# Expert steps 36 to 39 of a routed expert kernel put under run-time conditions on the number of steps in use

## The chip, the core and the metric

One core of one Trainium2 chip runs the whole program. The metric is the device time of one execution in microseconds; the kernel before has a median of 1045.79 us over three runs.

## What is computed

The input is q, k and v for 8 batches, 8 heads, 576 positions and 64 features per head. Attention acts within chunks of 64 positions. Its output, 4608 tokens of 512 features, goes through a router that sends each token to one of 8 experts, and through that expert's two layers. All data are fp32.

```python
# attention, per chunk of 64
scores = scale * q_c @ k_c.T;  attn = softmax(scores);  out = attn @ v_c
# bridge: (B, H, S, D) -> x of (4608, 512)
logits = normalised(x) @ normalised(expert_emb).T / tau
expert_idx = argmax(logits);  gate_w = probs[expert_idx]
for e in range(8):
    mask = expert_idx == e
    out[mask] = gate_w[mask] * (relu(x[mask] @ w1[e]) @ w2[e])   # 512 -> 1024 -> 512
```

## The kernel before

The program has three stages on the core. The **attention stage** works through 36 tiles of 128 tokens; it also forms the router's logits, and writes the attention output to the DRAM tensor `x_rows`. The **seam** sorts the tokens: it gives each token a block of 64 tokens of one expert, and each block a place in a step. The **expert stage** runs steps.

A step holds two blocks, one in each half of 128 rows. The blocks are numbered by expert; half 0 takes them from the front and half 1 from the back, so that `mid`, half the number of blocks rounded up, is the number of steps that have a block (lines 367 and 368). How many blocks there are depends on the data: 4608 tokens are 72 full blocks, and each expert's last block may be partly filled. The fixed number of steps is `NST = NT + E // 2` = 36 + 4 = 40. Steps from `mid` on hold padding: their gather reads row 0, and their scatter rows are out of range, so that nothing is written.

The seam also makes two small tables on one partition: `eblk`, the expert of each half in each step, and `fresh`, which is 1 where a step's expert differs from that of the step two before. SP reads both (`number`, line 483) and issues a weight load of a step and half only where `fresh` is set (`load_w`, line 494). Each weight buffer is double, by the step's parity.

A step consists of these parts:

- `gather` (line 513): POOL fetches 128 rows of `x_rows` by an indirect DMA, four steps ahead.
- `turn_xb` (line 525): PE transposes the rows, DVE copies them to `xbT` (line 531).
- `hidden` (line 534): 16 matmul calls of 512 columns, 32 instructions in the profile, on the first layer (line 541); DVE applies the relu to the first half of h (line 552) and ACT to the second (line 550).
- `turn_h` (line 555): eight transposes of h on PE (line 562), copied to `hT` by DVE (line 566) and ACT (line 564).
- `result` (line 569): 16 matmul calls on the second layer (line 574); ACT scales by the gate (line 582) and POOL scatters the rows to the output (line 583).

The order of the work is written out by hand (`manual_schedule`), and each engine runs its instructions in that order. The loop at line 604 is a software pipeline: in its turn j, PE does `hidden` of step j + 1, `turn_h` of j, `turn_xb` of j + 2 and `result` of j - 1. Nearly every wait of PE for DVE or ACT is thus filled with another step's matmuls. SP's queue holds the weight loads in the same order; a load waits until the matmuls that read its buffer are done.

Of the kernel before, what the change touches and what calls it, by code (L numbers as in the profile page):

```python
# [11 lines left out]
I32 = mybir.dt.int32  # L12
AF = mybir.ActivationFunctionType
ALU = mybir.AluOpType
AX = mybir.AxisListType
PSUM = bass.MemoryType.PSUM
ENG = mybir.EngineType
# [8 lines left out]
def kernel(  # L26
# [11 lines left out]
    nc = tc.nc  # L38
# [7 lines left out]
    NT = N // P  # L46
    NCB = S // CH
    G = P // 2
    NST = NT + E // 2
# [4 lines left out]
    keep = ctx.enter_context(tc.tile_pool(name="keep", bufs=1))  # L54
# [12 lines left out]
    gate_at = keep.tile([P, NST], FP32, name="gate_at")  # L67
    eblk = keep.tile([1, 2, NST], I32, name="eblk")
    fresh = keep.tile([1, 2, NST], I32, name="fresh")

    make_identity(nc, ident)

# [213 lines left out]
    with (  # L286
# [7 lines left out]
        io = sp.tile([P, P], FP32, name="io")  # L294
# [66 lines left out]
        mid = sp.tile([P, 1], FP32, name="mid")  # L361
# [28 lines left out]
        for i in range(2):  # L390
            nc.vector.tensor_scalar(
                fresh[:, i, 0:2], e_of[:, i, 0:2], float((0, E - 1)[i]), None, ALU.not_equal
            )
        nc.vector.tensor_tensor(
            fresh[:, :, 2:NST], e_of[:, :, 2:NST], e_of[:, :, 0 : NST - 2], ALU.not_equal
        )


# [75 lines left out]
    with (  # L474
# [5 lines left out]
    ):  # L480
        xin, mo = {}, {}

        def number(ap, top, engine):
            return nc.values_load(
                ap,
                engines=(engine,),
                min_val=0,
                max_val=top,
                skip_runtime_bounds_check_because="a count of comparisons, less than this",
            )  # L490
# [3 lines left out]
        def load_w(buf, rows, n, s, j):  # L494

            if (s, j) not in new:
                new[s, j] = (
                    number(eblk[0:1, s, j : j + 1], E - 1, ENG.SP),
                    number(fresh[0:1, s, j : j + 1], 1, ENG.SP),
                )  # L500
            e, f = new[s, j]
            nc.sync.dma_start(out=buf[s][j % 2], in_=rows[:, ds(e * n, n), :], cond=f > 0)

        def load_w1(j):
            for s in range(2):
                load_w(w1_sb, w1_rows, KD, s, j)

        def load_w2(j):
            for s in range(2):
                load_w(w2_sb, w2_rows, KF, s, j)  # L510
                del new[s, j]

        def gather(j):
            t = bp.tile([P, D], FP32, tag="xin", name="xin", bufs=XBUF)
            nc.gpsimd.indirect_dma_start(  # L515
                out=t,
                out_offset=None,
                in_=x_rows,
                in_offset=bass.IndirectOffsetOnAxis(ap=src_row[:, j : j + 1], axis=0),
                bounds_check=N - 1,  # L520
                oob_is_err=False,
            )
            xin[j] = t

        def turn_xb(j):
            t = xin.pop(j)
            ps = ps_x.tile([P, KD, P], FP32, tag="x", name="x_ps")
            for c in range(KD):
                nc.tensor.transpose(ps[:, c], t[:, c * P : c * P + P], ident)
            xT = bp.tile([P, KD, P], FP32, tag="xbT", name="xbT")  # L530
            nc.vector.tensor_copy(xT, ps)  # L531
            mo[j] = {"xT": xT}

        def hidden(j):
            d = mo[j]
            h = bp.tile([P, F], FP32, tag="h", name="h")
            for fh in range(F // 512):
                ps = ps_h.tile([P, 512], FP32, tag="h", name="h_ps")
                for c in range(KD):
                    for s in range(2):  # L540
                        nc.tensor.matmul(  # L541
                            ps[G * s : G * s + G],
                            lhsT=d["xT"][:, c, G * s : G * s + G],
                            rhs=w1_sb[s][j % 2][:, c, fh * 512 : fh * 512 + 512],
                            start=(c == 0),
                            stop=(c == KD - 1),
                        )
                dst = h[:, fh * 512 : fh * 512 + 512]
                if fh % 2:
                    nc.scalar.activation(dst, ps, AF.Relu)  # L550
                else:
                    nc.vector.tensor_scalar(dst, ps, 0.0, None, ALU.max)  # L552
            d["h"] = h

        def turn_h(j):
            d = mo[j]
            hT = bp.tile([P, KF, P], FP32, tag="hT", name="hT")
            for g in range(KF // 4):
                ps = ps_ht.tile([P, 4, P], FP32, tag="ht", name="ht_ps")
                for c in range(4):  # L560
                    f0 = (4 * g + c) * P
                    nc.tensor.transpose(ps[:, c], d["h"][:, f0 : f0 + P], ident)  # L562
                if g % 2:
                    nc.scalar.copy(hT[:, 4 * g : 4 * g + 4], ps)
                else:
                    nc.vector.tensor_copy(hT[:, 4 * g : 4 * g + 4], ps)  # L566
            d["hT"] = hT

        def result(j):
            d = mo.pop(j)  # L570
            ps = ps_y.tile([P, D], FP32, tag="y", name="y_ps")
            for c in range(KF):
                for s in range(2):
                    nc.tensor.matmul(  # L574
                        ps[G * s : G * s + G],
                        lhsT=d["hT"][:, c, G * s : G * s + G],
                        rhs=w2_sb[s][j % 2][:, c],
                        start=(c == 0),
                        stop=(c == KF - 1),
                    )  # L580
            y = bp.tile([P, D], FP32, tag="y", name="y", bufs=3)
            nc.scalar.activation(y, ps, AF.Copy, scale=gate_at[:, j : j + 1])  # L582
            ins = nc.gpsimd.indirect_dma_start(  # L583
                out=out,
                out_offset=bass.IndirectOffsetOnAxis(ap=dst_row[:, j : j + 1], axis=0),
                in_=y,
                in_offset=None,
                bounds_check=N - 1,
                oob_is_err=False,
            )  # L590
            tc.declare_no_dep(ins.ins, group="rows", reason="blocks hold different tokens")
            tc.add_to_no_dep_group("rows", ins.ins)
# [8 lines left out]
        hidden(0)  # L601
        load_w1(2)
        turn_xb(1)
        for j in range(NST + 1):
            if j + 1 < NST:
                hidden(j + 1)
                if j + 3 < NST:
                    load_w1(j + 3)
            if j < NST:
                turn_h(j)  # L610
            if j + 2 < NST:
                turn_xb(j + 2)
            if j > 0:
                result(j - 1)
                if j + 1 < NST:
                    load_w2(j + 1)
            if j + XBUF < NST:
                gather(j + XBUF)


# [26 lines left out]
```

## Time and profile before

| | |
|---|---|
| three runs | 1044.2, 1045.79, 1046.27 us; median 1045.79 |
| the profiled execution, in all | 1047.4 us |
| its span, first to last instruction | 1045.6 us |
| mean granted TensorE clock | 0.82 |
| PE busy | 907.6 us (87% of the span) |
| DVE, ACT, POOL busy | 268.5, 173.1, 103.9 us |
| DMA | 142.58 MB |

The profile is of one execution. PE is TensorE's matmuls and PEld its weight loads, DVE VectorE, ACT ScalarE, POOL GpSimd and SP the queue that issues weight loads. Times count from the start of the span. The granted clock is a share of full speed: 1.00 is 2.4 GHz and 0.50 is 1.2 GHz. L574 is line 574 of the kernel before. The busy share of the whole span says little here, since the attention stage, the seam and the expert stage have different limits; the rows below are therefore read by stretch.

### The profile page before, as it was taken

Reading aid. Unit: us, or ns where it says so; the run is one execution under the profiler, and the core shown is the slowest. Engines: PE = TensorE matmul, PEld = TensorE weight load, DVE = VectorE, ACT = ScalarE, POOL = GpSimd, SP = SyncE. Lnnn points to the kernel's source line nnn. Section 1 sums busy time; section 2 is a strip of 40 time slices with the busy share of each in tenths; the row PEclk is TensorE's granted clock in tenths of the full one; section 3 lists DMA queues with packets and bytes.
Section 4 is the critical chain, followed back from the end, with each engine's and each line's share of the span. In section 5 each row is a group of like instructions: output and inputs, shape, how many; then the busy total and the mean of one; then the engine's idle time right before and its main releaser. Section 6 shows DMA issues by size and latency. Waiting matters only on the chain.

```text
span 1045.6 us, 15287 instructions
## 1 busy us (share of the span) xinstructions
PE 907.6 (87%) x6287; PEld 485.3 (46%) x6287; DVE 268.5 (26%) x508; ACT 173.1 (17%) x310; POOL 103.9 (10%) x128
## 2 busy tenths in 40 slices
PE   4777777767777745899999999999999999999998
PEld 4666666656666635333333333333333333333332
DVE  3444444343444466111111111111111111111110
ACT  3222222222222220011111011011111101101111
POOL 0000000000000000101111101101110110111101
PEclk9855555555555555899999999999999999999999
DMA  8555465457374100101013575167942142316670
GB/s 204 147 150 168 113 185 171 116 162 200 88 207 133 40 21 1 51 19 41 21 41 121 202 261 202 41 226 285 345 162 106 51 186 106 121 41 233 229 256 2
DMA packets 153670, 142.58 MB, mean 136 GB/s; under 512 B 115702, under 2 KB 115702, under 8 KB 153600
## 3 DMA queue, kind: packets, MB, share of 16 engines
q1 hardware_dynamic: 144256, 112.21, 34.6%
q0 software_dynamic: 9344, 29.39, 7.9%
q8 instruction: 50, 0.82, 0.3%
q14 instruction: 20, 0.16, 0.0%
HBM read 391.14 MB, written 19.92 MB: 393 GB/s over the span
## 4 chain that ended last, share of the span: by engine, by line
issue 56%; PE 21%; DVE 14%; POOL 5%; ACT 2%; POOLq 0%; DMA 0%; SPq 0%
PE lg_ps L226 6%; PE tr L136 6%; PE sc L154 4%; POOL xin L515 4%; PE tr L181 3%; DVE mx L162 2%; DVE a L164 2%; DVE qT L141 2%; DVE rs L172 2%; ACT a L170 2%; DVE xT L220 2%; POOL out_dram L583 2%; PE inv L451 1%; DVE rs L173 1%; DMA kx<-in_k_dram 0%
## 5 line engine op out<-in xcount | busy, mean ns | idle before, releaser
L541 PE MATMUL h_ps<-w,xbT 128*64 128x512 f32 x1280 | 284.5, 597 | 2.4 <-DVE xbT L531 2.4
L574 PE MATMUL y_ps<-w,hT 128*64 128x512 f32 x1280 | 283.3, 595 | 0.0
L541 PEld LDWEIGHTS h_ps<-w,xbT 128*64 128x64 f32 x1280 | 92.3, 138 | 186.5 <-issue 183.3
L574 PEld LDWEIGHTS y_ps<-w,hT 128*64 128x64 f32 x1280 | 88.5, 137 | 167.0 <-issue 167.0
L552 DVE TENSOR_SCALAR h<-h_ps 128x512 f32<-128x512 f32 x40 | 27.7, 692 | 377.9 <-PE h_ps L541 377.9
L226 PE MATMUL lg_ps<-enT,xT 128*128 128x8 f32 x288 | 64.2, 352 | 62.3 <-DVE xT L220 62.3
L583 POOL DMA_INDIRECT out_dram<-y,dst_row x40 | 40.6, 1014 | 532.6 <-ACT y L582 517.2
L226 PEld LDWEIGHTS lg_ps<-enT,xT 128*128 128x128 f32 x288 | 60.8, 312 | 69.2 <-DVE xT L220 69.1
L582 ACT ACTIVATE y<-y_ps,gate_at 128x512 f32<-128x512 f32 x40 | 27.5, 688 | 272.9 <-PE y_ps L574 272.9
L550 ACT ACTIVATE h<-h_ps 128x512 f32<-128x512 f32 x40 | 23.9, 598 | 285.1 <-PE h_ps L541 285.1
L154 PE MATMUL sc<-kT,qT 64*64 64x64 f32 x1152 | 40.7, 317 | 31.5 <-DVE qT L141 31.5
L566 DVE COPY hT<-ht_ps 128x512 f32<-128x512 f32 x40 | 27.7, 692 | 136.6 <-PE ht_ps L562 136.6
L141 DVE COPY qT<-tr 128x512 f32<-128x512 f32 x36 | 24.9, 691 | 136.5 <-PE tr L136 136.5
L154 PEld LDWEIGHTS sc<-kT,qT 64*64 64x64 f32 x1152 | 35.0, 218 | 44.9 <-issue 42.4
L209 POOL DMA_DIRECT2D x_rows<-x x36 | 19.6, 544 | 352.3 <-DVE x L202 352.3
L562 PEld LDWEIGHTS ht_ps<-ident,h 128*128 128x128 f32 x320 | 34.3, 140 | 32.5 <-issue 32.5
L515 POOL DMA_INDIRECT xin<-x_rows,src_row x40 | 41.0, 1024 | 49.5 <-DVE dst_row L465 37.6
L170 ACT ACTIVATE a<-a 128x512 f32<-128x512 f32 x36 | 22.7, 630 | 132.5 <-DVE a L164 132.5
L562 PE MATMUL ht_ps<-ident,h 128*128 128x128 f32 x320 | 43.7, 280 | 0.0
L194 PE MATMUL sc<-v,aT 64*64 64x64 f32 x1152 | 40.8, 318 | 0.0
L136 PE MATMUL tr<-ident,kx 128*128 128x128 f32 x144 | 36.4, 405 | 4.9 <-DMA kx<-in_k_dram 4.9
L218 PE MATMUL tr<-ident,x 128*128 128x128 f32 x144 | 40.0, 433 | 0.0
(118 smaller groups left out, 605.4 us busy)
## 6 DMA issues: line engine op xcount, KB each, us to landing
w<-in_moe_w_dram SPq DMA_DIRECT2D x168, 2048.0 KB
v<-in_v_dram SPq DMA_DIRECT2D x64, 144.0 KB
x_rows<-x POOLq DMA_DIRECT2D x36, 256.0 KB, 2.3
qx<-in_q_dram SPq DMA_DIRECT2D x32, 256.0 KB
kx<-in_k_dram SPq DMA_DIRECT2D x32, 256.0 KB
qx<-in_q_dram SPq DMA_DIRECT2D x8, 128.0 KB
kx<-in_k_dram SPq DMA_DIRECT2D x8, 128.0 KB
xin<-x_rows,src_row POOLq DMA_INDIRECT x40, 3.5
```

The source lines that it names most:

```text
L136: nc.tensor.transpose(ps[:, i], a[:, i * P : i * P + P], ident)
L141: nc.vector.tensor_copy(x, ps)
L154: nc.tensor.matmul(sc[CH * c : CH * c + CH, par, i], lhsT=qx[r0 : r0 + CH, i, c0 : c0 + CH], rhs=kx[r0 : r0 + CH, i, c0 : c0 + CH], start= ...
L170: nc.scalar.activation(a, a, AF.Exp, scale=scale)
L194: nc.tensor.matmul(pv[CH * c : CH * c + CH, par, i], lhsT=d["aT"][r0 : r0 + CH, i, CH * c : CH * c + CH], rhs=v_t[b][r0 : r0 + CH, i, cb], ...
L218: nc.tensor.transpose(ps[:, c], d["x"][:, c * P : c * P + P], ident)
L226: nc.tensor.matmul(lg_ps[:, t], lhsT=d["xT"][:, c], rhs=enT[:, c], start=(c == 0), stop=(c == KD - 1),)
L515: nc.gpsimd.indirect_dma_start(out=t, out_offset=None, in_=x_rows, in_offset=bass.IndirectOffsetOnAxis(ap=src_row[:, j : j + 1], axis=0), ...
L541: nc.tensor.matmul(ps[G * s : G * s + G], lhsT=d["xT"][:, c, G * s : G * s + G], rhs=w1_sb[s][j % 2][:, c, fh * 512 : fh * 512 + 512], sta ...
L562: nc.tensor.transpose(ps[:, c], d["h"][:, f0 : f0 + P], ident)
L574: nc.tensor.matmul(ps[G * s : G * s + G], lhsT=d["hT"][:, c, G * s : G * s + G], rhs=w2_sb[s][j % 2][:, c], start=(c == 0), stop=(c == KF ...
L583: ins = nc.gpsimd.indirect_dma_start(out=out, out_offset=bass.IndirectOffsetOnAxis(ap=dst_row[:, j : j + 1], axis=0), in_=y, in_offset=Non ...
```

## The change

The seam now also keeps `mid` as an integer, `n_steps`, and multiplies `fresh` by `used`, which is 1 for steps below `mid`. The pipelined loop covers steps 0 to 35 (`LEAST = NT` = 36); its prefetches of weights and its gathers still reach into the steps behind it. After the loop, all five engines load `n_steps` into a register. Then step 36 stands in a condition on `n_steps > 36`, and inside it, behind step 36, step 37 in a condition on `n_steps > 37`, and so on to 39. In a condition the parts of a step follow each other without another step's work between them.

```diff
+    n_steps = keep.tile([1, 1], I32, name="n_steps")
...
+        used = sp.tile([1, NST], I32, name="used")
+        nc.vector.tensor_scalar(used, io[0:1, 0:NST], mid[0:1], None, ALU.is_lt)
+        nc.vector.tensor_copy(n_steps, mid[0:1])
         nc.vector.tensor_tensor(
             fresh[:, :, 2:NST], e_of[:, :, 2:NST], e_of[:, :, 0 : NST - 2], ALU.not_equal
+        )
+        nc.vector.tensor_tensor(
+            fresh, fresh, used.unsqueeze(1).to_broadcast([1, 2, NST]), ALU.mult
         )
...
-        def number(ap, top, engine):
+        def number(ap, top, *engines):
             return nc.values_load(
                 ap,
-                engines=(engine,),
+                engines=engines,
...
-        for j in range(NST + 1):
-            if j + 1 < NST:
+
+        LEAST = NT
+        for j in range(LEAST + 1):
+            if j + 1 < LEAST:
                 hidden(j + 1)
                 if j + 3 < NST:
                     load_w1(j + 3)
-            if j < NST:
+            if j < LEAST:
                 turn_h(j)
-            if j + 2 < NST:
+            if j + 2 < LEAST:
                 turn_xb(j + 2)
             if j > 0:
                 result(j - 1)
...
+        steps = number(n_steps, NST, ENG.PE, ENG.DVE, ENG.Activation, ENG.Pool, ENG.SP)
+
+        def more(j):
+            with tc.If(steps > j):
+                turn_xb(j)
+                hidden(j)
+                if j + 2 < NST:
+                    load_w1(j + 2)
+                turn_h(j)
+                result(j)
+                if j + 2 < NST:
+                    load_w2(j + 2)
+                if j + 1 < NST:
+                    more(j + 1)
+
+        more(LEAST)
```

The added lines shift the numbers behind them: what was L531, L541, L550, L552, L562, L564, L566, L574, L582 and L583 is L538, L548, L557, L559, L569, L571, L573, L581, L589 and L590 in the changed kernel.

On PE, where x of step 36 is turned, the order before is this; `h_ps` is written by the matmuls of `hidden` (here of step 35), `ht_ps` by the transposes of h (step 34), and `y_ps` by `result` (step 33):

```order
L541 MATMUL h_ps<-w_01_61,xbT 64x512
L541 MATMUL h_ps<-w_11_63,xbT 64x512
L562 MATMUL ht_ps<-ident,h 128x128 x8
L529 MATMUL x_ps<-ident,xin 128x128 x4
L574 MATMUL y_ps<-w_01_65,hT 64x512
L574 MATMUL y_ps<-w_11_67,hT 64x512
```

In the changed kernel it is this, the first two rows being the last ones of result 35:

```order
L581 MATMUL y_ps<-w_01_65,hT 64x512
L581 MATMUL y_ps<-w_11_67,hT 64x512
L491 TENSOR_LOAD n_steps
L632 COMPARE_AND_BRANCH
L536 MATMUL x_ps<-ident,xin 128x128 x4
L548 MATMUL h_ps<-w_00_60,xbT 64x512
L548 MATMUL h_ps<-w_10_62,xbT 64x512
```

The transposes of step 36's x moved from between two other steps' matmuls to behind the last result of the loop, a register load and a branch, and its `hidden` follows them directly.

In the seam on DVE, the order before and then that of the change (`io` counts 0, 1, 2, ... along a row, `e_of` holds the experts of the steps):

```order
L391 TENSOR_SCALAR fresh<-e_of 1x2 x2
L394 TENSOR_TENSOR fresh<-e_of 1x2x38
L403 TENSOR_TENSOR w<-rank,off 128x288
L404 TENSOR_TENSOR w<-w,eq 128x288
L405 TENSOR_REDUCE dest<-w 128x36
```

```order
L392 TENSOR_SCALAR fresh<-e_of 1x2 x2
L396 TENSOR_SCALAR used<-io,mid 1x40
L397 CAST n_steps<-mid 1x1
L398 TENSOR_TENSOR fresh<-e_of 1x2x38
L401 TENSOR_TENSOR fresh<-fresh,used 1x80
L410 TENSOR_TENSOR w<-rank,off 128x288
L411 TENSOR_TENSOR w<-w,eq 128x288
L412 TENSOR_REDUCE dest<-w 128x36
```

Three operations on one partition now stand ahead of the chain from `w` on.

At the program's end on POOL, before and then in the changed kernel:

```order
L515 DMA xin<-x_rows,src_row 128x512
L583 DMA out_dram<-y,dst_row 4608x512 x5
L642 UNCONDITIONAL_BRANCH
L642 ISA
```

```order
L522 DMA xin<-x_rows,src_row 128x512
L590 DMA out_dram<-y,dst_row 4608x512
L491 TENSOR_LOAD n_steps
L632 COMPARE_AND_BRANCH
L590 DMA out_dram<-y,dst_row 4608x512
L632 COMPARE_AND_BRANCH
L590 DMA out_dram<-y,dst_row 4608x512
```

Of the five scatters behind the last gather, one is left ahead of the register load, and each of the four others stands behind a branch of its own. The part for a condition that does not hold stands further down: it sets the semaphores to what the skipped steps would have left, and branches to the end of the program.

## Rows read from the trace of the kernel before

**Rows 1.** Busy time by stretch: us, PE, PEld, DVE, ACT, POOL, PEclk, DMA share, GB/s

```profile
433.00:450.00 17.00, 15.43 (x78) 5.71 (x76) 3.46 (x5) 1.62 (x3) 0.00 (x0) 1.00 0.00 1
450.00:1000.00 550.00, 550.00 (x2726) 208.07 (x2726) 74.54 (x108) 67.41 (x108) 72.43 (x71) 1.00 0.41 146
```

**Rows 2.** Timeline of the last steps: start us, duration us, engine, line, operation

```profile
987.39 1.09 PE L562 MATMUL ht_ps<-ident,h 128*128 128x128 f32 x8
...
987.58 0.60 ACT L550 ACTIVATE h<-h_ps 128x512 f32<-128x512 f32 x1 [6.22 <-PE h_ps L541]
988.14 0.69 DVE L566 COPY hT<-ht_ps 128x512 f32<-128x512 f32 x1 [3.32 <-PE ht_ps L562]
...
995.77 7.04 PE L541 MATMUL h_ps<-w,xbT 128*64 128x512 f32 x32
...
1018.08 1.09 PE L562 MATMUL ht_ps<-ident,h 128*128 128x128 f32 x8
...
1027.14 13.95 PE L574 MATMUL y_ps<-w,hT 128*64 128x512 f32 x64
```

**Rows 3.** The same view, POOL alone, 1000 us to the end

```profile
1012.32 1.00 POOL L583 DMA_INDIRECT out_dram<-y,dst_row  x1 [14.33 <-ACT y L582]
...
1042.16 0.98 POOL L583 DMA_INDIRECT out_dram<-y,dst_row  x1 [5.93 <-ACT y L582]
```

**Rows 4.** DMA, 1011 to 1020 us: packets, MB, share; issues, us to landing

```profile
q1 hardware_dynamic: 1047, 2.11, 69.4%
q0 software_dynamic: 80, 0.13, 3.8%
...
out_dram<-y,dst_row POOLq DMA_INDIRECT x1, 6.8
```

**Rows 5.** The same view, 1035 to 1040 us

```profile
q0 software_dynamic: 80, 0.00, 0.8%
...
out_dram<-y,dst_row POOLq DMA_INDIRECT x1, 2.1
```

**Rows 6.** Timeline at the head of the expert stage, PE and DVE

```profile
441.94 0.60 PE L529 MATMUL x_ps<-ident,xin 128*128 128x128 f32 x4
...
442.57 0.69 DVE L531 COPY xbT<-x_ps 128x512 f32<-128x512 f32 x1 [0.18 <-PE x_ps L529]
443.32 7.09 PE L541 MATMUL h_ps<-w,xbT 128*64 128x512 f32 x32 [0.78 <-DVE xbT L531]
...
450.34 1.09 PE L562 MATMUL ht_ps<-ident,h 128*128 128x128 f32 x8
```

**Rows 7.** Busy time by stretch, columns as in rows 1, around the loads for step 36

```profile
990.00:995.00 5.00, 5.00 (x26) 1.67 (x24) 0.00 (x0) 0.00 (x0) 0.00 (x0) 1.00 0.05 20
```

**Rows 8.** Timeline of DVE in the seam, operations on one partition

```profile
387.98 0.19 DVE L388 TENSOR_SCALAR e_of<-e_of 1x80 f32<-1x80 f32 x1
388.20 0.19 DVE L389 CAST eblk<-e_of 1x80 int32<-1x80 f32 x1
388.31 0.22 DVE L391 TENSOR_SCALAR fresh<-e_of 1x2 int32<-1x2 f32 x2
```

**Rows 9.** Timeline of PE from the seam into the expert stage

```profile
399.79 15.65 PE L451 MATMUL inv<-rr,oh 128*128 128x80 f32 x72 [14.60 <-DVE oh L450]
420.75 1.09 PE L529 MATMUL x_ps<-ident,xin 128*128 128x128 f32 x4 [5.30 <-DMA xin<-x_rows,src_row]
422.62 10.00 PE L541 MATMUL h_ps<-w,xbT 128*64 128x512 f32 x32 [0.78 <-DVE xbT L531]
```

**Rows 10.** Instructions of L484: duration ns min/median/max, first and last start us

```profile
L484 SPq TENSOR_LOAD <-fresh x80: 261/266/278, 389.0 to 987.9; - x80
```

**Rows 11.** Instructions of L642, the program's end, columns as in rows 10

```profile
L642 PEldq DRAIN  x2: 13/2256/4498, 1036.7 to 1045.2; - x2
```

**Rows 12.** DMA issues, 459.5 to 472 us, columns as in rows 4

```profile
xin<-x_rows,src_row POOLq DMA_INDIRECT x1, 3.4
```

**Rows 13.** The page's DMA queues: packets, MB, share of 16 engines

```profile
q8 instruction: 50, 0.82, 0.3%
```

## The prediction

> **What bounds the kernel now.** Steps are numbered from 0, so the change keeps steps 0 to 35 as they are and puts 36, 37, 38 and 39 under conditions. I read four views, in this order.
>
> First the busy time by stretch [rows 1]. From 450 to 1000 us TensorE is busy for 550.00 of 550 us at a granted clock of 1.00, its upper level of 2.4 GHz, with DMA at a share of 0.41. The expert stage is TensorE's alone: what a step is worth there is its time on PE.
>
> Then the timeline of the last steps on PE [rows 2]. The transposes of h (L562) of step 36 start at 987.39 and those of step 38 at 1018.08, so a step takes (1018.08 - 987.39) / 2 = 15.345 us. The last results, of steps 38 and 39, run together from 1027.14 for 13.95 us, to 1041.09: 6.98 each. Then come ACT's scaling, the last scatter on POOL at 1042.16 [rows 3], its landing and the closing barrier, to 1045.6.
>
> Third, which steps have work at all. POOL issues four scatters at the end, of steps 36 to 39, the first at 1012.32 and the last at 1042.16 [rows 3]. The first one moves 0.13 MB [rows 4], which is 64 rows of 2 KB: one half of a step. The third moves 0.00 MB [rows 5]; the second and fourth show the same zero. So 37 steps are in use, step 36 with one half filled, and steps 37, 38 and 39 compute padding only. The changed kernel should run step 36 and skip three.
>
> Last, the place where a step runs alone, as the conditional ones will: the head of the expert stage [rows 6], read below.
>
> **The change, part by part.** *Four pipelined steps go.* The loop now ends at 36 steps, with the same drain at its end (a step without a next x to turn, one without a next hidden, a last result), so it ends four periods earlier: 4 x 15.345 = 61.38 us less. Call the end of the 36th result T; it was 1041.09 and would be 979.71.
>
> *One step comes back, unpipelined.* The conditional step writes turn_xb, hidden, turn_h and result in a row, so PE waits for DVE twice where the old loop had another step's matmuls to put in between. Row by row:
> - x turned until hidden starts: 443.32 - 441.94 = 1.38 [rows 6], of which 0.78 is the wait for DVE's copy of xbT.
> - hidden until turn_h starts: 450.34 - 443.32 = 7.02 [rows 6].
> - turn_h until result starts: DVE's copy of the first half of hT starts 988.14 - 987.39 = 0.75 after turn_h and takes 0.69 [rows 2], and PE answers a DVE copy 443.32 - (442.57 + 0.69) = 0.06 later [rows 6]: 1.50. The second four transposes must also wait for ACT's relu of the second half of h, which ends (987.58 + 0.60) - 987.39 = 0.79 after turn_h's start [rows 2]; that still lies inside the 1.50.
> - result: 6.98 [rows 2]. ACT's copy of the second half of hT is wanted 3.5 us into it and hides.
>
> Together 16.88 us, so PE ends at T + 16.88, and 61.38 - 16.88 = 44.50 us less than before. Weights don't stop this. The later of the two loads for step 36, w2, starts once result 34 is over; before, that is when hidden of step 37 starts, one period ahead of hidden of step 38: 995.77 - 15.35 = 980.4 [rows 2]. DMA stands at a share of 0.05 between 990 and 995 [rows 7], so the load took at most some 10 to 11 us. Now PE wants it for result 36, one result and 1.38 + 7.02 + 1.50 us later: 16.88 us after its start. The x of steps 36 to 39 is still gathered in the fixed loop.
>
> *Three small DVE operations in the seam.* `used`, `n_steps` and the product into `fresh` work on one partition. Neighbours there start 0.11 us apart, and 0.22 apart where one reads the other's result [rows 8]: 0.11 + 0.11 + 0.22 = 0.44 us, between 0.2 and 0.7. It counts in full: PE's next matmuls wait 14.60 us for DVE, and the first gather after them holds PE for another 5.30 [rows 9], so nothing hides a later DVE.
>
> *Register load and branch on all five engines.* A load of a number into a register takes 0.27 us on SP [rows 10]; on the other engines the trace has none, and of branches none at all. PE has a cover for it: its sequencer reached the closing DRAIN 4.50 us before the array was done [rows 11], so it runs ahead, and load plus branch lie beside the last result's matmuls. DVE finished its last copy for the loop long before T. ACT has scaled result 35 by T + 1.07 (1042.16 - 1041.09, when POOL takes it [rows 3]), and is next wanted for the relu at T + 8.4. SP and POOL have nothing that step 36 waits for before its scatter. At the exit SP and POOL jump twice, beside the scatter's landing. Bounds: 0 if all of it is covered, 6.2 if two code fetches stand open one behind the other (3.1 each, worked out in the first rival). I take 0.3, one register load left open, because the cover of 4.50 is far over 0.27. The Trainium skill, "Advanced Engine Details and Errata", section Control Flow Timing, gives about 108 ns for a compare-and-branch and 51 ns for a branch; by that alone the term would be about 0.2 us, an estimate from the page, and no run here shows it yet.
>
> *The last scatter now has rows.* Before, the last scatter was empty and an empty one landed 2.1 us after its issue [rows 5]. Now it is step 36's, with 64 rows. The same one took 6.8 us before [rows 4], but beside 2.11 MB of weights [rows 4] that steps 37 to 39 had asked for; `fresh` times `used` takes such loads away. The nearest quiet row is a gather of 128 rows, 3.4 us [rows 12]. I take 2.9, near the middle of 2.1 and 3.4: 0.8 us more, between 0 and 4.7.
>
> **The sum.** -61.38 + 16.88 + 0.44 + 0.3 + 0.8 = -42.96 us. The profiled execution took 1047.4 us in all, of which 1045.6 are its span; it is 1.6 above the median of the three runs, 1045.79. All terms lie inside the span, so the like of the profiled execution would take 1004.4 and the median becomes **1002.8 us**. About 0.2%, some 2 us, is what a measurement of this kernel can tell from no change.
>
> **Rivals.**
> *Code fetch stands open at the exit or entry.* The instruction queue moved 50 pieces in 0.3% of 16 engines' span [rows 13]: 0.003 x 16 x 1045.6 / 50 = 1.0 us each, and a DMA without data takes 2.1 from issue to landing [rows 5], so one fetch is about 3.1 us. PE jumps over three unused step bodies, SP and POOL over short ones. One fetch left open in place of the 0.3 gives 1005.6, two 1008.7. Against it: the covers named above. The Trainium skill, "Runtime: NRT & Kernel Launch", section Instruction fetch mechanics, says that a taken branch outside the prefetched window must fetch its target before execution goes on; by that rule this rival holds wherever the cover is shorter than the fetch. No branch in this trace bears it out or denies it. Chance 0.24.
>
> *PE's clock falls at the branch.* If PE's sequencer loses its lead and the array idles for some 2 to 5 us at the condition, step 36 may start at the lower level. At the head of the stage, after 5.30 us of idling, PE turned x in 1.09 instead of 0.60 and took 10.00 instead of 7.09 for its first hidden [rows 6, 9]: 3.4 us more. With the gap, 1008 to 1011.5. Against it: the gaps of 0.78 us between 433 and 450 left the clock at 1.00 [rows 1]; the conditional step's own gaps are of that size. Chance 0.05.
>
> *More steps are in use than I read.* Each further step run costs 16.88: 38 steps give about 1019.7, 39 about 1036. Against it: the empty scatters [rows 5]. Chance 0.02.
>
> *Slower: all 40 steps run* (the number comes out as 40, or the conditions skip nothing). Four steps at 16.88 replace four at 15.345, +6.14, and with the seam's 0.44 and 0.3 for each of four conditions about 1053.6. This decides from 40 steps in use on, since 39 would still gain 9. The number is computed from the same `mid` by which the rows are laid out, and the rows left the last three steps empty. Chance 0.02.
>
> **How the numbers follow.** The forecast has 0.67; its own range is 1001 to 1005, from the bounds of seam (0.2 to 0.7), scatter (mostly 2.1 to 3.4) and small branch costs. The low end of the range, 1000.8, takes the lower bounds of all three (1001.5) and a run a little under the median, as 1044.2 was. The high end, 1008.7, takes in the first rival with two fetches. Beyond it lie most of the second rival and the two others, and below it little. All cases but the last are faster by far more than 0.2%: faster 0.97, within 0.2% 0.01, slower 0.02.
>
> **What would show it.** In the profile of the changed kernel: 37 instead of 40 in the counts of L538, L557 and L590 (L531, L550 and L583 before); one step period from the last pipelined result's end to the last result's end of about 17 us, with PE waiting 0.78 for xbT and some 0.5 to 0.7 for hT; no gap on PE before the conditional x transposes; the granted clock at 1.00 to the end; fewer bytes on SP's queue at the end, as the loads for steps 37 to 39 go; the last scatter landing in about 2.9. A PE gap of over 1 us at the condition, a tail longer than about 6 us after the last result, or 40 in the counts would prove me wrong, each for its own rival.

## The result and the profile after

| | before | changed |
|---|---|---|
| median of 4 runs, us | 1044.99 | 1011.87 |
| lowest to highest, us | 1043.94 to 1046.27 | 1009.90 to 1013.82 |
| profiled execution: time, span, us | 1047.4, 1045.6 | 1009.90, 1008.1 |
| TensorE's last matmul to the span's end, us | 4.55 | 14.40 |

The profiled execution of the kernel before is not one of its four runs; that of the changed kernel is the lowest of its four. The ratio is 0.9682, with a 95% interval of 0.9654 to 0.9711. The kernel is faster by 33.1 us; 43 were forecast, and 1011.87 lies 3.2 above the range's upper end.

The page's list of costly groups, and the page's first part for PE, show that the part meant to go is gone. The columns of a group are busy time, mean ns of one and idle time before it.

```profile
PE 857.2 (85%) x6059; PEld 464.1 (46%) x6059; DVE 262.7 (26%) x502; ACT 167.5 (17%) x301; POOL 101.0 (10%) x125
...
L590 POOL DMA_INDIRECT out_dram<-y,dst_row x37 | 37.6, 1016 | 489.9 <-ACT y L589 473.9
...
L210 POOL DMA_DIRECT2D x_rows<-x x36 | 19.6, 544 | 350.2 <-DVE x L203 350.2
L522 POOL DMA_INDIRECT xin<-x_rows,src_row x40 | 41.0, 1024 | 50.0 <-DVE dst_row L472 38.1
```

The same groups of the kernel before:

```profile
L583 POOL DMA_INDIRECT out_dram<-y,dst_row x40 | 40.6, 1014 | 532.6 <-ACT y L582 517.2
...
L209 POOL DMA_DIRECT2D x_rows<-x x36 | 19.6, 544 | 352.3 <-DVE x L202 352.3
...
L515 POOL DMA_INDIRECT xin<-x_rows,src_row x40 | 41.0, 1024 | 49.5 <-DVE dst_row L465 37.6
```

The scatters are 37, so one conditional step ran and three were skipped. The other two groups matter further on: 36 row writes, 40 gathers, 37 scatters and two single loads (of the router's embedding and of tau) are all the DMAs that POOL issues, 115 in the changed kernel. Before, with 40 scatters, it issued 118.

The timeline of the changed kernel, from the last two pipelined results on PE to the last scatter on POOL (start, duration, engine, line):

```profile
962.81 13.95 PE L581 MATMUL y_ps<-w,hT 128*64 128x512 f32 x64
...
976.69 0.66 PE L536 MATMUL x_ps<-ident,xin 128*128 128x128 f32 x4
...
977.38 0.69 DVE L538 COPY xbT<-x_ps 128x512 f32<-128x512 f32 x1 [14.16 <-PE x_ps L536]
...
978.13 7.09 PE L548 MATMUL h_ps<-w,xbT 128*64 128x512 f32 x32 [0.78 <-DVE xbT L538]
...
985.15 1.45 PE L569 MATMUL ht_ps<-ident,h 128*128 128x128 f32 x8
...
986.64 7.09 PE L581 MATMUL y_ps<-w,hT 128*64 128x512 f32 x32
...
993.85 0.69 ACT L589 ACTIVATE y<-y_ps,gate_at 128x512 f32<-128x512 f32 x1 [6.59 <-PEq L632]
...
994.82 1.01 POOL L590 DMA_INDIRECT out_dram<-y,dst_row  x1 [15.96 <-ACTq L632]
```

PE goes from the last pipelined result (962.81 + 13.95 = 976.76) into the conditional step without a gap and ends at 986.64 + 7.09 = 993.73. The busy time by stretch, columns as in [rows 1], shows what follows:

```profile
976.00:994.00 18.00, 16.77 (x80) 5.67 (x76) 2.08 (x3) 2.02 (x4) 1.02 (x1) 1.00 0.25 95
994.00:1008.10 14.10, 0.00 (x0) 0.00 (x0) 0.00 (x0) 0.54 (x1) 1.01 (x1) 0.63 0.03 10
```

The clock stays at 1.00 to PE's end. Then 14 us pass in which the core computes nothing: one ACT operation (the rest of ACT's scaling), one scatter, DMA at a share of 0.03. That scatter is not what is waited for; it lands 2.9 us after its issue. This is the DMA view, 994 to 1000 us:

```profile
out_dram<-y,dst_row POOLq DMA_INDIRECT x1, 2.9
```

The instructions of two lines tell what is. L632 is the condition, L668 the program's end; columns are count, duration ns min/median/max, first and last start. In the changed kernel:

```profile
L632 PEldq COMPARE_BRANCH  x3: 92/192/3441, 972.9 to 994.0; - x3
...
L632 POOLq INC_SWDGE_SEM  x1: 2505/2505/2505, 995.1 to 995.1; - x1
```

```profile
L668 SPq EVENT_SEMAPHORE  x14: 17/28/73, 997.6 to 1008.1; - x14
...
L668 POOLq DRAIN  x3: 51/99/9458, 997.8 to 1007.8; - x3
```

And the program's end in the kernel before:

```profile
L642 POOLq DRAIN  x3: 51/99/2766, 1041.9 to 1045.4; - x3
```

After the scatter POOL first executes INC_SWDGE_SEM, which stands in the part for a condition that does not hold, for 2.5 us. Then its closing DRAIN, an instruction that every engine's queue has at the program's end, stands for 9.46 us, from 997.8 to 1007.3; the program's last semaphore events follow it. Before, it started ahead of the last scatter's end and took 2.77. Set against the end of the last scatter's issue, the DRAIN ended 1041.9 + 2.77 - (1042.16 + 0.98) = 1.5 us later before [rows 3], and 997.8 + 9.46 - (994.82 + 1.01) = 11.4 us later now (1.55 and 11.47 from unrounded times). This difference of 9.9 us accounts for the whole growth of the tail, from 4.55 to 14.40.

### The profile page after: what moved, and what is told of

The parts are those of the page before. It is cut to its first block, busy times and chain, and to the rows that moved or that the text cites. A ratio compares the mean times of both kernels' runs of the same rounds, so it can differ in the third digit from the quotient of the medians.

```text
span 1008.1 us, 14792 instructions
## 1 busy us (share of the span) xinstructions
PE 857.2 (85%) x6059; PEld 464.1 (46%) x6059; DVE 262.7 (26%) x502; ACT 167.5 (17%) x301; POOL 101.0 (10%) x125
## 4 chain that ended last, share of the span: by engine, by line
PE 77%; DVE 15%; issue 3%; ACT 3%; DMA 1%; POOL 0%; SPq 0%; POOLq 0%
PE y_ps L581 25%; PE h_ps L548 25%; PE lg_ps L227 6%; PE tr L137 6%; PE sc L155 4%; PE ht_ps L569 4%; PE tr L182 3%; DVE mx L163 3%; DVE a L165 3%; DVE qT L142 3%; DVE rs L173 2%; ACT a L171 2%; DVE xT L221 2%; PE x_ps L536 2%; PE inv L458 2%
## 5 line engine op out<-in xcount | busy, mean ns | idle before, releaser
L548 PE MATMUL h_ps<-w,xbT 128*64 128x512 f32 x1184 | 262.2, 595 | 3.1 <-DVE xbT L538 3.1
L581 PE MATMUL y_ps<-w,hT 128*64 128x512 f32 x1184 | 262.0, 595 | 0.0
L548 PEld LDWEIGHTS h_ps<-w,xbT 128*64 128x64 f32 x1184 | 85.0, 138 | 172.3 <-issue 168.0
L581 PEld LDWEIGHTS y_ps<-w,hT 128*64 128x64 f32 x1184 | 81.8, 137 | 154.6 <-issue 154.3
L559 DVE TENSOR_SCALAR h<-h_ps 128x512 f32<-128x512 f32 x37 | 25.6, 692 | 341.4 <-PE h_ps L548 341.4
L590 POOL DMA_INDIRECT out_dram<-y,dst_row x37 | 37.6, 1016 | 489.9 <-ACT y L589 473.9
L589 ACT ACTIVATE y<-y_ps,gate_at 128x512 f32<-128x512 f32 x37 | 25.4, 688 | 252.1 <-PE y_ps L581 245.5
L557 ACT ACTIVATE h<-h_ps 128x512 f32<-128x512 f32 x37 | 22.1, 598 | 266.6 <-PE h_ps L548 266.6
L573 DVE COPY hT<-ht_ps 128x512 f32<-128x512 f32 x37 | 25.6, 692 | 126.3 <-PE ht_ps L569 122.9
L569 PEld LDWEIGHTS ht_ps<-ident,h 128*128 128x128 f32 x296 | 31.7, 141 | 30.4 <-issue 30.0
L569 PE MATMUL ht_ps<-ident,h 128*128 128x128 f32 x296 | 40.7, 280 | 0.1
```

The source lines that it names most:

```text
L548: nc.tensor.matmul(ps[G * s : G * s + G], lhsT=d["xT"][:, c, G * s : G * s + G], rhs=w1_sb[s][j % 2][:, c, fh * 512 : fh * 512 + 512], sta ...
L581: nc.tensor.matmul(ps[G * s : G * s + G], lhsT=d["hT"][:, c, G * s : G * s + G], rhs=w2_sb[s][j % 2][:, c], start=(c == 0), stop=(c == KF ...
L590: ins = nc.gpsimd.indirect_dma_start(out=out, out_offset=bass.IndirectOffsetOnAxis(ap=dst_row[:, j : j + 1], axis=0), in_=y, in_offset=Non ...
```

## Experiments

Twelve kernels, in four groups. The table has what each left in its profile. "DRAIN" is the long one of POOL at the program's end; its end is counted from the end of POOL's last issue, as just worked out; "tail" is from the last matmul's end to the span's end.

| kernel | time, us | POOL's DMAs | DRAIN, us | its end after the last issue, us | tail, us |
|---|---|---|---|---|---|
| before | 1044.99 | 118 | 2.77 | 1.55 | 4.55 |
| changed | 1011.87 | 115 | 9.46 | 11.47 | 14.40 |
| e1, one condition | 1010.13 | 115 | 10.29 | 9.47 | 12.40 |
| e2, 37 fixed steps | 1014.09 | 115 | 10.70 | 9.46 | 12.63 |
| e3, two conditions | 1012.38 | 115 | 9.46 | 11.37 | 14.29 |
| e4, scatters outside | 1004.51 | 118 | 3.30 | 2.08 | 5.22 |
| f1, e2 and three gathers | 1007.44 | 118 | 3.32 | 2.08 | 5.54 |
| f2, before less three gathers | 1056.84 | 115 | 10.68 | 9.47 | 12.62 |
| f3, e2 and one gather | 1010.58 | 116 | 3.23 | 1.99 | 7.29 |
| f4, e1 and a copy on POOL | 1010.72 | 115 | 10.29 | 9.47 | 12.41 |
| g1, e2 less three gathers | 1008.49 | 112 | 10.44 | 9.22 | 12.07 |
| g2, e2 less one gather | 1012.54 | 114 | 10.61 | 9.38 | 12.54 |
| g3, changed and three gathers | 1003.99 | 118 | 2.45 | 2.08 | 5.29 |
| h1, e1 and row writes by ACT | 1006.10 | 79 | 7.60 | 6.52 | 9.45 |

The changed kernel, e1 to e4 and g3 have medians of four runs, the f, the other g and h1 a single one. The kernel before ran at a median of 1046.47 beside e1 to e4, 1044.79 beside the f, 1044.2 beside the g, and 1044.85 beside h1. The first `hidden` of the expert stage starts anywhere from 420.9 (e1) to 425.0 us (f1) in these profiles, in a stretch that most of the edits do not touch, and single times move with it; so the readings below go by the DRAIN and the tail.

### Is it the conditions? e1, e2, e3, e4

The first suspicion was the conditions themselves: that skipped scatters cost POOL time at the exit (A), or that a branch on POOL does (B).

e1 leaves the condition on step 36 alone:

```diff
                 if j + 2 < NST:
                     load_w2(j + 2)
-                if j + 1 < NST:
-                    more(j + 1)
```

> The kernel has the condition on step 36 alone; steps 37 to 39 are left out of the program, so nothing is skipped. Theory A (POOL's instruction that stands in for the skipped scatters, INC_SWDGE_SEM, and the DRAIN that waits for it make the long tail): the branches are taken but that instruction does not run, POOL's last DRAIN is about 3 to 3.5 us instead of 9.5, the tail after the last result about 5.5 instead of 14.4, the time about 1003. Theory B (a run-time branch on POOL, or code fetched for it, makes the tail): DRAIN stays near 9.5 and the time near 1012.

The ratio was 0.9652 (0.9628 to 0.9677). No INC_SWDGE_SEM is executed, and the tail fell by 2.0 us, to 12.40; but the DRAIN alone still ends 9.47 us after the last issue. So A carries 2 us and no more: skipping is not what makes the DRAIN long.

e2 has no condition at all:

```diff
-        LEAST = NT
+        LEAST = NT + 1
...
-        more(LEAST)
```

> No conditions at all: 37 pipelined steps, steps 37 to 39 left out. What is left to gain without any branch: 1045.0 - 3 x 15.345 + 0.5 for the seam + 0.8 for the last scatter's rows = about 1000.3 by all theories, unless theory D holds (a last scatter that writes rows, in place of an empty one, lengthens POOL's last DRAIN): then DRAIN is near 9.5 and the time about 1007.

The ratio was 0.9674 (0.9641 to 0.9708). The program's end in e2:

```profile
L652 POOLq DRAIN  x3: 51/99/10704, 1002.1 to 1013.6; - x3
```

A program without any condition has the same long DRAIN, which ends 9.46 us after the last issue. A and B both fall as its cause. Theory D, that a last scatter which writes rows makes the DRAIN long, is left by this run; it falls below with e4, whose last scatter writes the same rows ahead of a short DRAIN, and with f2, whose last scatter is empty ahead of a long one. A wait that was not expected came with it. The last two results in e2's timeline:

```profile
981.93 7.94 PE L581 MATMUL y_ps<-w,hT 128*64 128x512 f32 x34
...
992.57 8.72 PE L581 MATMUL y_ps<-w,hT 128*64 128x512 f32 x30 [2.70 <-DMA w<-in_moe_w_dram]
```

Result 36 follows result 35 directly here, and 2.70 us pass in waiting for its weights, which come 11.6 us after the end of result 34 (980.98 to 992.57; the forecast took 10 to 11). Then the granted clock, 1.00 from 980 to 990 us, was 0.75 from 990 to 995 and 0.94 from 995 to 1002, and 30 matmuls took 8.72 us where 32 take 7.09. These two costs, and not only the tail, lie between e2's 1014.09 and the 1000.3 that was expected without theory D. In the conditional order result 36 starts 9.88 us after the end of result 35 (986.64 - 976.76) and does not wait: the forecast was right that the weights are there in time, but the pipelined order has no such slack.

e3 keeps the conditions of steps 36 and 37:

```diff
-                if j + 1 < NST:
+                if j < LEAST + 1:
                     more(j + 1)
```

> Conditions on steps 36 and 37 only, so the skipped part stands in for one scatter and not for three. Theory A1 (the cost grows with the number of scatters stood in for, 2.5 + 9.5 us for three): about 4 us for one, nearly hidden by the scatter's landing; tail about 6.5, time about 1004. Theory A2 (the cost is fixed): INC_SWDGE_SEM and DRAIN as before, time about 1012. Theory B: 1012 as well, with the long DRAIN in the kernel with one condition too.

The ratio was 0.9667 (0.9641 to 0.9693). The instructions of L632 in e3:

```profile
L632 POOLq INC_SWDGE_SEM  x1: 2484/2484/2484, 997.7 to 997.7; - x1
```

One skipped scatter costs as much as three (2.48 against 2.51 us), so this price is not per scatter (A2, not A1).

e4 keeps all conditions, and takes the four scatters behind them, in the order 39, 38, 37, 36. The tiles that they read are zeroed at the start; step 36's is scaled by ACT, those of 37 to 39 by DVE:

```diff
+            if j < NT:
+                y = bp.tile([P, D], FP32, tag="y", name="y", bufs=3)
+                nc.scalar.activation(y, ps, AF.Copy, scale=gate_at[:, j : j + 1])
+                scatter(j, y)
+            elif j == NT:
+                nc.scalar.activation(yc[0], ps, AF.Copy, scale=gate_at[:, j : j + 1])
+            else:
+                nc.vector.tensor_scalar(yc[j - NT], ps, gate_at[:, j : j + 1], None, ALU.mult)
...
         more(LEAST)
+        for j in range(NST - 1, LEAST - 1, -1):
+            scatter(j, yc[j - NT])
```

> All four conditions stand, but the four scatters of steps 36 to 39 stand behind them and always run, those of 39, 38 and 37 first, so that POOL has nothing to stand in for; steps 37 to 39 are scaled by DVE instead of ACT. Theory A: no INC_SWDGE_SEM, the three empty scatters lie beside result 36, tail about 5.5 us, time about 1003. Theory B: the branches are all there, the tail stays near 14 and the time near 1012.

The ratio was 0.9595 (0.9571 to 0.9620): faster than the changed kernel, with a tail of 5.22. POOL's last four issues in e4's timeline:

```profile
992.06 1.01 POOL L602 DMA_INDIRECT out_dram<-yc,dst_row  x1 [8.06 <-DVEq L644]
995.21 1.00 POOL L602 DMA_INDIRECT out_dram<-yc,dst_row  x1 [2.15 <-issue]
996.52 0.99 POOL L602 DMA_INDIRECT out_dram<-yc,dst_row  x1 [0.30 <-issue]
999.90 0.98 POOL L602 DMA_INDIRECT out_dram<-yc,dst_row  x1 [2.39 <-ACTq L644]
```

With e4 and the kernel before on one side, and e1 to e3 and the changed kernel on the other, one number parts them: 118 DMAs issued by POOL against 115. But e4 also keeps POOL busy just before the end, and the 118 of both end in scatters. The next runs part these.

### Is it the count, or what POOL does at the end? f1 to f4

In the expectations that follow, N is the theory that the number of POOL's DMAs decides, R that POOL's last microseconds do. f1 takes e2 and adds three spare gathers early in the stage, far from the end; f3 adds one:

```diff
+            if j in EXTRA:
+                nc.gpsimd.indirect_dma_start(
+                    out=spare,
...
+                    in_offset=bass.IndirectOffsetOnAxis(ap=src_row[:, 0:1], axis=0),
```

with `EXTRA = (10, 14, 18)` in f1 and `(10,)` in f3.

> The kernel with 37 fixed steps and no condition, with three gathers into a spare tile added in steps 10, 14 and 18, so that POOL issues 118 DMAs again as in the kernel before, while its last ones stay as they are. What is measured is how long POOL's closing DRAIN lasts after the last scatter's issue: 9.5 us with 115 DMAs in all, 1.6 and 2.1 us in the two kernels with 118. Theory N (the number of DMAs that POOL has issued in all decides): about 2 us. Theory R (what POOL did in the last microseconds decides: the kernels with a short DRAIN had other scatters 1 to 7 us before the last one, the others nothing for 11 to 16 us): 9.5 us.

The program's end in f1:

```profile
L664 POOLq DRAIN  x3: 51/99/3315, 1000.9 to 1005.4; - x3
```

Three more DMAs, issued hundreds of us earlier, took the DRAIN from 10.70 to 3.32 us and the tail from 12.63 to 5.54. N, the count, holds here, and R does not.

f2 takes the kernel before and leaves out the gathers of steps 37 to 39:

```diff
             if j + XBUF < NST:
-                gather(j + XBUF)
+                if j + XBUF < NT + 1:
+                    gather(j + XBUF)
+                else:
+                    xin[j + XBUF] = last[0]
```

> The kernel before with its 40 steps, but without the gathers of steps 37 to 39, which read the rows of step 36 instead (their scatters write nothing in any case): 115 DMAs on POOL, and three empty scatters at the end as before, 6 to 7 us apart. Theory N: the closing DRAIN lasts 9.5 us after the last issue and the span grows by about 8. Theory R: 1.6 us, span unchanged.

The program's end in f2:

```profile
L646 POOLq DRAIN  x3: 51/99/10681, 1043.3 to 1054.8; - x3
```

The kernel before, with three DMAs fewer and nothing added, ran 12.05 us longer than its neighbour (1056.84 against 1044.79). 8.1 of it are the tail, 12.62 against 4.55 in the profile of before. Of the other 4, 1.3 are a later start of the expert stage than in that profile; the neighbour itself has no profile. The long DRAIN is neither the change's nor the conditions': it follows the count both ways.

> As the kernel with three more gathers, but with one more, in step 10: 116 DMAs. Theory N: the DRAIN takes another value, or one of the two; it is 9.5 us if the count must pass a bound above 116. Theory R: 9.5 us.

One gather more, the 116th DMA, is enough to make the DRAIN short, at 3.23 us. But the tail is 7.29, not 5.54 as in f1. POOL's last issue in f3's timeline:

```profile
1004.09 1.01 POOL L593 DMA_INDIRECT out_dram<-y,dst_row  x1 [13.08 <-issue]
```

PE ended at 1001.54, so this scatter, the 116th DMA itself, starts 2.55 us after it; in e2 the last one started 1.06 after PE (1002.34 - 1001.28). Something of 1.5 us comes before the 116th. The second row of e4 shows it too, where the 116th started 2.15 after the one before instead of 0.30. In f1 and g3 the 116th is a gather, the last one, and starts 2.17 after the one before. This is f1's:

```profile
986.50 1.03 POOL L525 DMA_INDIRECT xin<-x_rows,src_row  x1 [2.17 <-issue]
```

The kernel before shows it as well, whose 116th is the scatter of step 37. Its timeline:

```profile
1026.27 0.69 ACT L582 ACTIVATE y<-y_ps,gate_at 128x512 f32<-128x512 f32 x1 [6.42 <-PE y_ps L574]
...
1028.72 1.00 POOL L583 DMA_INDIRECT out_dram<-y,dst_row  x1 [15.40 <-ACT hT L564]
```

It starts 1.76 us after its ACT operation's end (1026.96), where the scatter of step 39 starts 0.28 after its own (1042.16 - 1041.88). There, and in f1 and g3, the delay hid behind work of PE that was still to come.

f4 takes e1 and has POOL copy a tile of h during step 36, so that POOL does not idle for 16 us ahead of the last scatter:

```diff
             d["hT"] = hT
+            if j == LEAST:
+                nc.gpsimd.tensor_copy(spare, hT[:, 0])
```

> The kernel with the condition on step 36 alone (nothing skipped, no INC_SWDGE_SEM, DRAIN 9.5 us after the last issue), with one copy of 128x128 by POOL added when hT of step 36 is ready, some 7 us before the last scatter; 115 DMAs. Theory R in the form that POOL's idling before the last scatter decides: about 2 us. Theory N: 9.5 us. R in the form that only another DMA shortly before helps: 9.5 us too.

DRAIN and tail are e1's (10.29 and 12.41). That POOL idles before the last scatter does not matter.

### How does it depend on the count? g1, g2, g3, h1

g1 takes e2 without the gathers of steps 37 to 39, g2 without that of 39:

```diff
-            if j + XBUF < NST:
+            if j + XBUF < LEAST:
                 gather(j + XBUF)
```

(`NST - 1` in place of `LEAST` in g2). Theory L says that every count up to 115 gives the long DRAIN, theory P that it is the 115th DMA behind which POOL's next action is dear. The first expectation is g1's, and "the kernel with one fewer" in it is g2.

> As the kernel with one fewer, without the gathers of steps 37, 38 and 39: 112 DMAs. Theory P: about 2 us. Theory L: 9.5 us, or more, if the DRAIN works off what is left up to a bound near 115.

> The kernel with 37 fixed steps and no condition, without the gather of step 39, whose rows nothing reads: 114 DMAs on POOL. Theory P (the 115th DMA is a point at which POOL's next action is dear, as the 116th starts late in the kernel before): DRAIN about 2 us after the last issue. Theory L (every count up to 115 gives the long DRAIN): 9.5 us.

The last issue and the program's end in g1, two views, and then in g2:

```profile
995.59 0.98 POOL L590 DMA_INDIRECT out_dram<-y,dst_row  x1 [8.13 <-ACT y L589]
```

```profile
L652 POOLq DRAIN  x3: 51/99/10436, 995.4 to 1006.3; - x3
```

```profile
999.22 0.99 POOL L590 DMA_INDIRECT out_dram<-y,dst_row  x1 [7.95 <-ACT y L589]
```

```profile
L652 POOLq DRAIN  x3: 51/99/10609, 999.0 to 1010.1; - x3
```

The DRAIN ends 9.22 us after the last issue with 112 DMAs, 9.38 with 114 and 9.47 with 115. That is 9.22 / 112 = 0.0823, 9.38 / 114 = 0.0823 and 9.47 / 115 = 0.0823 us for each DMA issued by POOL: L holds, P falls. A list that is worked off one entry at a time would look so; that there is one is not shown.

g3 adds the three spare gathers, in steps 10, 14 and 18, to the changed kernel itself, with all its conditions.

> The changed kernel, all four conditions and the skipped part as they are, with three gathers into a spare tile added in steps 10, 14 and 18, where POOL idles: 118 DMAs run on POOL instead of 115. Theory N (the number of DMAs that POOL has run decides on its closing DRAIN): the DRAIN falls from 9.5 to about 2 us behind INC_SWDGE_SEM, the tail from 14.4 to about 7, the time from 1011.9 to about 1004.5. If skipping itself costs (theory A), the time stays near 1012.

The ratio was 0.9611 (0.9592 to 0.9631), a median of 1003.99. The condition and the program's end in g3, two views:

```profile
L643 POOLq INC_SWDGE_SEM  x1: 404/404/404, 995.7 to 995.7; - x1
```

```profile
L679 POOLq DRAIN  x3: 51/105/2447, 996.3 to 999.6; - x3
```

Three transfers that nothing reads take the changed kernel's tail from 14.40 to 5.29. Against their own runs of before, the changed kernel is 33.1 us faster and g3 40.2 (1044.2 - 1003.99): 7.1 more. INC_SWDGE_SEM shrinks with the DRAIN, from 2.51 to 0.40 us.

h1 moves the 36 row writes of the attention stage from POOL's queue to ACT's, in e1, which leaves POOL 79:

```diff
-            nc.gpsimd.dma_start(out=x_rows[P * t : P * t + P, :], in_=x)
+            nc.scalar.dma_start(out=x_rows[P * t : P * t + P, :], in_=x)
```

> The kernel with the condition on step 36 alone, with the 36 writes of the attention output to x_rows issued by ACT instead of POOL, so that POOL issues 79 DMAs instead of 115. Theory L in its measured form: the closing DRAIN ends 9.22, 9.38 and 9.47 us after the last issue with 112, 114 and 115 DMAs, which is 0.0823 us for each DMA and nothing besides; for 79 it must be 6.50 us. If instead the long DRAIN has a fixed part and a small slope near the bound, it stays above 8 us; if it is tied to a count near 115 alone, it is 2.

The program's end in h1:

```profile
L666 POOLq DRAIN  x3: 51/105/7602, 995.9 to 1004.0; - x3
```

The DRAIN ended 995.9 + 7.60 - (995.96 + 1.00) = 6.5 us after the last issue; 79 x 0.0823 is 6.50. The line through 112 to 115 holds 36 DMAs lower, though those 36 are direct writes and g1 and g2 left out indirect gathers. Of the versions run four times, e4 and g3 beat both kernels; their intervals overlap. e4 issues the same 118 DMAs at any number of steps. g3's count is 118 at 37 steps in use and 117 at 36, and grows by one with each further step.

## Why the prediction was right or wrong

The span went from 1045.64 to 1008.13, by 37.51 us; the forecast's sum was 42.96. Step by step:

- **Four periods, -61.38: right.** From the end of the first hidden to the end of the last pipelined result the stage is shorter by just that. Before, the first hidden ended at 422.62 + 10.00 [rows 9] and the last result at 1041.09 [rows 2]: 608.47. Now the first hidden, in the timeline of PE, ended at 420.94 + 8.72 and result 35 at 976.76: 547.10. The difference is 61.37.
- **The conditional step, +16.88: right.** It measured 993.73 - 976.76 = 16.97, its parts 978.13 - 976.69 = 1.44 (1.38), 985.15 - 978.13 = 7.02 (7.02), 986.64 - 985.15 = 1.49 (1.50) and 7.09 (6.98). Its weights were there.
- **The seam, +0.44: right.** The timeline of DVE in the changed kernel:

```profile
386.18 0.22 DVE L392 TENSOR_SCALAR fresh<-e_of 1x2 int32<-1x2 f32 x2
386.32 0.23 DVE L396 TENSOR_SCALAR used<-io,mid 1x40 int32<-1x40 f32 x1
386.47 0.13 DVE L397 CAST n_steps<-mid 1x1 int32<-1x1 f32 x1
386.54 0.21 DVE L398 TENSOR_TENSOR fresh<-e_of 1x76 int32<-1x76 f32 x1
386.78 0.23 DVE L401 TENSOR_TENSOR fresh<-fresh,used 1x80 int32<-1x80 int32 x1
386.94 0.44 DVE L410 TENSOR_TENSOR w<-rank,off 128x288 f32<-128x288 f32 x1
```

From L392 to L410 0.76 us pass. Before, L391 started at 388.31 [rows 8] and the same operation on `w` at 388.60, 0.29 later: 0.47 more.
- **Load and branch, +0.3: covered, no cost seen on PE.** PE's sequencer branched at 972.9, 3.8 us before the array was done with result 35. The price of a code fetch in the first rival was near right: PE's jump out of the conditions took 3.44 us against 3.1, and the instruction queue moved one piece of 0.02 MB within it; the same jump took 0.35 us in e3, where it passes one unused step body instead of three. It began at 989.29 and ended at 992.73, under result 36, which ran to 993.73. So the rival fell by its cover, not by its size. The Trainium skill, "Runtime: NRT & Kernel Launch", section Instruction fetch mechanics, says that a taken branch beyond the prefetched window waits for its target; this row agrees.
- **The last scatter's landing, +0.8: right in itself, and not what counts.** It landed after 2.9 us, as taken, but the kernel ends 12.3 us after that scatter's issue has ended.
- **The end of the program: the step that failed.** The prediction wrote "Then come ACT's scaling, the last scatter on POOL at 1042.16 [rows 3], its landing and the closing barrier, to 1045.6", and carried this stretch over from the kernel before, 4.55 us with 0.8 and 0.3 added, as 5.6 us. It measured 14.40, 8.8 more. The three skipped scatters, which the sum counted as nothing but saved work, took POOL's DMAs from 118 to 115, and so from a DRAIN of 1.55 us past the last issue to one of 9.47; INC_SWDGE_SEM added 2.0. The test named for this, a tail longer than about 6 us, did show it, but "each for its own rival" had only the code fetch for it: every rival that lengthened the time placed it in PE's path or in the sequencers', and none in what POOL does at the end.

The sum closes: 5.45 us less was saved in the profiled span than forecast (42.96 - 37.51). The tail's 8.8, with 0.1 for step and seam, is offset by 3.4 us at the start: the first hidden began 1.68 earlier though the seam grew by 0.47, so 2.15 come from a stage that the change does not touch, and it took 1.28 less (8.72 for 10.00) as the granted clock from 420 to 430 us was 0.79 instead of 0.57. Such a start differs from run to run and is luck here; the profiled execution is the lowest of the four, and the median, 1011.87, lies 9.1 above the forecast.

With the count restored the measured gain comes near the forecast's sum of 42.96: e4 is 41.96 us below its runs of before (1046.47 - 1004.51), and g3 40.2.

**The other rivals.** The clock did not fall: 1.00 from 976 to 994. The row from which its price was read shows no fall either: in the kernel before the granted clock was 0.50 already from 400 to 420 us. A fall behind a wait of PE is what e2 had. More than 37 steps, or all 40, did not run: 37 scatters.

## What to carry to other kernels

When a change takes work off an engine, look at that engine's rows at the program's end as well as at the end of the path: here POOL, busy for a tenth of the span, decided 8 to 10 us after TensorE was done. Count the DMAs that POOL issues before and after an edit, and where a short closing DRAIN becomes long, try a run with a few more or fewer of them, far from the end; it costs a few lines and tells the count apart from the edit's other effects. A conditional part costs little on TensorE when its sequencer reaches the branch ahead of the array, but what the condition skips on other queues is a change of its own.

## What the runs showed of the hardware that was not expected

- **POOL's closing DRAIN.** In these kernels it ended 0.0823 us per POOL DMA after the last issue: 6.52 at 79 DMAs, 9.22 at 112, 9.38 at 114, 9.47 at 115 (and 11.4 to 11.5 where INC_SWDGE_SEM stood ahead of it). With 116 and 118 it ended 1.99 to 2.08 us after, and 1.55 in the kernel before, whose last scatter is empty. The 116th DMA itself started some 1.5 to 1.9 us late in all five kernels that have one (the kernel before, e4, f1, f3, g3). What is counted, and whether the price builds up again beyond 118, no run shows.
- **INC_SWDGE_SEM.** Where the DRAIN was long it took 2.48 us for one skipped scatter (e3) and 2.51 for three; where the DRAIN was short it took 0.40, for three (g3). Why is open.
- **Branches.** On DVE, ACT, POOL and SP a compare-and-branch took 38 to 67 ns, on PE 92 and 192, and 3441 where the jump went past three unused step bodies (348 past one, in e3). The Trainium skill, "Advanced Engine Details and Errata", section Control Flow Timing, gives about 108 ns for a compare-and-branch; the rows here lie below it on four engines and on both sides of it on PE.
- **Still open:** why the wait for the weights of result 36 is 2.70 us in e2 and 3.2 in f3 but 1.0 to 1.9 in f1, g1 and g2, and what moves the start of the expert stage by up to 4 us between profiles.
